# Loading the first MLP weight's 128 half rows as the kernel's very first transfer, into a tile of their own

## Chip, cores and metric

The kernel runs on one core of a Trainium2 chip. The metric is the device time of one execution in microseconds. The time before is 189.7 us, the median of 3 runs (189.7 to 190.16).

## What is computed

A decode step for 8 batch rows: attention over the last 1024 cached positions, and an MLP, mixed by a gate.

```python
# x: 8 x 1 x 448; k_cache, v_cache: 8 x 8 x 4096 x 256; wq: 448 x 4096; wo: 4096 x 448
q = (x @ wq).reshape(B, Sq, 16, 256).transpose(0, 2, 1, 3)
k = repeat(k_cache[:, :, Sk - W:, :], 2, axis=1)          # W = 1024
v = repeat(v_cache[:, :, Sk - W:, :], 2, axis=1)
p = softmax(einsum("bhqd,bhkd->bhqk", q, k) * 256 ** -0.5)
a = einsum("bhqk,bhkd->bhqd", p, v).transpose(0, 2, 1, 3).reshape(B, Sq, 4096) @ wo
h = gelu(layernorm(x) @ w1 + b1)                          # w1: 448 x 1792
b = h @ w2 + b2                                           # w2: 1792 x 448
out = sigmoid((x * gate_w).sum(-1)) * a + (1 - sigmoid(...)) * b
```

All tensors are bfloat16.

## The kernel before

**The work.** `query` (L384) multiplies x by wq. Then, per batch row b, `transpose_keys` (L352) turns that row's keys on TensorE (a part by DVE and POOL, `turn_blocks`, L337), `scores` (L430) multiplies them by the query, the steps `top`, `expo`, `turn`, `scale` and `bring` make the softmax, and `values` (L502) multiplies the weights by the values. At the end `mlp_hidden` (L551) computes the MLP's hidden layer, and a last run of matmuls (L661 to L686) multiplies it by w2, and the attention's output by wo, into one sum.

**The loads.** Nearly everything large goes through one ring of four slots (`RING`, L69) of 32 KB per partition. `plan` is the list of loads in order: wq, the keys of row 0, then keys and values of each row in turn, `w12` (w1, and later w2), the last values, and wo (L162 to L177). `pump` (L98) issues loads as long as a slot is free, and `done` (L104), called when a slot's last reader is in place, issues the next. All of these are issued by SP, in this order, each as a few DMAs: `rows_loader` (L137) copies pieces side by side, `half_loader` (L115) and `pair_loader` (L125) load keys and values. Only x and the gate's weights are issued by ACT (L182, L186), and SP issues the biases between loads (L190). The order of instructions is written by hand (`manual_schedule`, L80); the framework adds the semaphore waits. A DMA takes one of a few completion semaphores in turn ("lanes"), so that a load also waits for an older load of its lane.

**The 448 rows of a weight.** 384 of them are three rows per partition, which load as one block. The remaining 64 rows are cut into halves, so that 128 half rows fill 128 partitions: `wq_t` (4096 B per partition) and `w1_t` (1792 B, L150). The matmuls over half rows use a stationary operand of their own (`ends`, L327): L402 for the query, L568 for the MLP. In the kernel before, slot `w12` holds w1's block, then w1's half rows from element `OW1T`, then w2 from element `OW2` (L153, L154). w2 is loaded behind the last values (`last_values`, L158).

Of the kernel before, what the change touches and what calls it, by code (L numbers as in the profile page):

```python
# [11 lines left out]
BF16 = mybir.dt.bfloat16  # L12
# [5 lines left out]
def kernel(  # L18
# [15 lines left out]
    nc = tc.nc  # L34
    P = nc.NUM_PARTITIONS
# [18 lines left out]
    FQ = F // QD  # L54
    FB = FQ // BL
    HH = HD // 2
    FH = F // 2
# [23 lines left out]
    consts = ctx.enter_context(tc.tile_pool(name="consts", bufs=1))  # L81
# [16 lines left out]
    def pump():  # L98
        while len(slots) < min(len(plan), consumed[0] + RING):
            t = ring.tile([P, SLOT], BF16, tag="slot", name="slot")  # L100
            plan[len(slots)](t)
            slots.append(t)
# [5 lines left out]
    def add(key, loader):  # L108
        index[key] = len(plan)
        plan.append(loader)  # L110

    def slot(*key):
        return slots[index[key]]

    def half_loader(src, b):  # L115
        def load(t):
            for i in range(NG):
                v = src[b, i:Hkv:NG, kv_base:Sk, :].rearrange(
                    "a (s c) d -> s a (c d)", c=NCK
                )  # L120
                nc.sync.dma_start(t[:, i * HS : (i + 1) * HS], v)

        return load

    def pair_loader(src, b, cuts=1):  # L125
        def load(t):
            n = HS // cuts
            tv = t[:].rearrange("p (i n) -> p i n", i=NG)
            v = src[b, :, kv_base:Sk, :].rearrange("h (s c) d -> s h (c d)", c=NCK)
            for k in range(cuts):  # L130
                nc.sync.dma_start(
                    tv[:, :, k * n : (k + 1) * n], v[:, :, k * n : (k + 1) * n]
                )

        return load

    def rows_loader(pieces):  # L137
        def load(t):
            o = 0
            for ap in pieces:  # L140
                n = ap.shape[-1]
                nc.sync.dma_start(t[:, o : o + n], ap)
                o += n

        return load

    wq_m = A_wq[0:DM, :].rearrange("(p r) n -> p (r n)", r=NR)
    wq_t = A_wq[DM:D, :].rearrange("r (h n) -> (r h) n", h=2)
    w1_m = B_w1[0:DM, :].rearrange("(p r) f -> p (r f)", r=NR)
    w1_t = B_w1[DM:D, :].rearrange("r (h n) -> (r h) n", h=2)  # L150
    w2_v = B_w2.rearrange("(p c) n -> p (c n)", c=FB)
    wo_v = A_wo.rearrange("(q p j) n -> p q (j n)", p=P, j=J8)
    OW1T = NR * F  # L153
    OW2 = OW1T + FH  # L154
    wq_r = [wq_m[:, 0:HD], wq_m[:, HD : NR * HD]]
    OWQ = HD // 2

    def last_values(t):  # L158
        pair_loader(A_v_cache, NB - 1, 2)(t)
        nc.sync.dma_start(slot("w12")[:, OW2 : OW2 + FB * D], w2_v)  # L160

    add(("wq",), rows_loader([wq_t] + wq_r))  # L162
    add(("k", 0), half_loader(A_k_cache, 0))
    for b in range(1, NB):
        add(("k", b), (half_loader if b == NB - 1 else pair_loader)(A_k_cache, b))
        add(("v", b - 1), pair_loader(A_v_cache, b - 1))
    add(("w12",), rows_loader([w1_m, w1_t]))
    add(("v", NB - 1), last_values)
    cuts = [(q, 0, J8) for q in range(NQW - 2)] + [
        (NQW - 2, 0, 4),  # L170
# [7 lines left out]

    x_sb = consts.tile([NB, D], BF16)
    consts.tile([P, SHIFT], F32, name="shift")  # L180
    pump()
    nc.scalar.dma_start(x_sb[:], xf)  # L182
    g_b = consts.tile([NB, D], BF16)
# [139 lines left out]
    def stationary(a, r):  # L323
        o = (a * NX + r) * GAP + BL
        return flat[:, o : o + NB]

    def ends(a, x2):  # L327
        o = (a * NX + NR) * GAP
        m = GAP + NB + BL * x2
        o += 0 if x2 else BL  # L330
        return flat[:, o : o + m], m
# [219 lines left out]
    def mlp_hidden():  # L551
        nc.vector.memset(hp[:], 0.0)
        w = slot("w12")
        for r in range(NR):
            for t in range(QD):
                o = r * F + t * FQ
                nc.tensor.matmul(
                    hp[BL * t : BL * t + NB, :],
                    lhsT=stationary(1, r),
                    rhs=w[:, o : o + FQ],  # L560
                    start=(r == 0),
                    stop=False,
                    skip_group_check=True,
                )
        for x2 in range(2):
            lhsT, m = ends(1, x2)
            o = OW1T + x2 * FQ
            nc.tensor.matmul(  # L568
                hp[0:m, :],
                lhsT=lhsT,  # L570
                rhs=w[:, o : o + FQ],
                start=False,
                stop=(x2 == 1),
                skip_group_check=True,
            )
        z = work.tile([P, FQ], F32, tag="w0", name="z")
        nc.vector.tensor_tensor(z[:], hp[:], b1_b[:], op=ALU.add)
        za = work.tile([P, FQ], F32, tag="w1", name="za")
        nc.vector.tensor_tensor(za[:], z[:], z[:], op=ALU.mult)
        zb = work.tile([P, FQ], F32, tag="w2", name="zb")  # L580
        nc.vector.tensor_scalar(
            zb[:], za[:], 0.044715, 1.0, op0=ALU.mult, op1=ALU.add
        )
        nc.vector.tensor_tensor(za[:], zb[:], z[:], op=ALU.mult)  # L584
        nc.scalar.activation(zb[:], za[:], ACT.Tanh, scale=0.7978845608028654)  # L585
        nc.vector.tensor_scalar(za[:], zb[:], 1.0, 0.5, op0=ALU.add, op1=ALU.mult)
        nc.vector.tensor_tensor(zb[:], za[:], z[:], op=ALU.mult)
        zt = work.tile([P, FB, BL], F32, tag="w3", name="zt")
        nc.vector.transpose(zt[:], zb[:].rearrange("p (e c) -> p c e", c=FB))
        hs = consts.tile([P, FB, NB], BF16)  # L590
        nc.vector.tensor_tensor(
            hs[:],
            zt[:, :, 0:NB],
            oall[:].rearrange("p (o b) -> p o b", o=1).to_broadcast([P, FB, NB]),
            op=ALU.mult,
        )
        return hs
# [25 lines left out]
    for b in range(1, NB):  # L623
# [9 lines left out]
    spread(b - 1)  # L633
    bring(b)
    hs = mlp_hidden()
    values(b)
    finish(b)
# [5 lines left out]
    w = slot("wo")  # L643
    NCH = NQW * J8
    chunks = [
        (hs[:, c, :], w2[:, OW2 + c * D : OW2 + (c + 1) * D]) for c in range(FB)
    ] + [(oP[:, c % J8, c // J8, :], w[:, c * D : (c + 1) * D]) for c in range(NCH)]
# [13 lines left out]
    for i, (lhsT, rhs) in enumerate(wide):  # L661
# [4 lines left out]
            rhs=rhs,  # L666
# [9 lines left out]
    for i, (lhsT, rhs) in enumerate(narrow):  # L676
        k = part[i]
        for h in range(2):
# [4 lines left out]
                rhs=rhs[:, h * DO : (h + 1) * DO],  # L683
# [39 lines left out]
```

## Time and profile before

| | |
|---|---|
| median of 3 runs | 189.7 us (189.7 to 190.16) |
| profiled execution, its own time | 189.85 us |
| span in its profile | 188.1 us |
| PE busy | 119.9 us (64%) |
| DVE busy | 95.3 us (51%) |
| ACT busy | 90.8 us (48%) |
| POOL busy | 67.1 us (36%) |
| read from HBM | 77.69 MB, 413 GB/s over the span |
| w1's half rows | 1 DMA of 224 KB |

How to read the profile: all times are microseconds from the span's start, if they are not marked ns. The row of 40 digits gives an engine's busy share in 40 equal slices of the span, in tenths; 9 is 90% or more. The DMA row is the mean over the core's 16 DMA engines, and the row under it what they moved. Queue q1 is SP's, q10 ACT's, and q8 and q14 fetch instructions. A timeline line is: start, duration, engine, line, operation, output <- input, count, and in brackets how long the engine had been idle and what ended that. An "SPq" line is the issuing of a DMA, not the transfer. The chain that ended last is followed back from the last instruction, at each step to what released it. The trace also holds a record of each DMA packet: its start, duration, size and queue, though not its engine.

### The profile page before, as it was taken

Reading aid. Unit: us, or ns where it says so; the run is one execution under the profiler, and the core shown is the slowest. Engines: PE = TensorE matmul, PEld = TensorE weight load, DVE = VectorE, ACT = ScalarE, POOL = GpSimd, SP = SyncE. Lnnn points to the kernel's source line nnn. Section 1 sums busy time; section 2 is a strip of 40 time slices with the busy share of each in tenths; the row PEclk is TensorE's granted clock in tenths of the full one; section 3 lists DMA queues with packets and bytes.
Section 4 is the critical chain, followed back from the end, with each engine's and each line's share of the span. In section 5 each row is a group of like instructions: output and inputs, shape, how many; then the busy total and the mean of one; then the engine's idle time right before and its main releaser. Section 6 shows DMA issues by size and latency. Waiting matters only on the chain.

```text
span 188.1 us, 2798 instructions
## 1 busy us (share of the span) xinstructions
PE 119.9 (64%) x1103; PEld 78.7 (42%) x1104; DVE 95.3 (51%) x166; ACT 90.8 (48%) x115; POOL 67.1 (36%) x143
## 2 busy tenths in 40 slices
PE   0255078778778396890684959943968885353772
PEld 0013077476357135650663457614853662110221
DVE  7304543664287726840682228824763773762511
ACT  2003879489469426941295129820891994010000
POOL 8000075093069605800398029101991840000000
PEclk9999859969999759997599678996699999955899
DMA  6999999999999999999999999999999999999991
GB/s 219 446 422 435 432 432 425 435 428 428 432 434 425 427 428 428 439 425 428 428 439 422 439 425 432 428 435 425 432 428 435 428 428 419 417 427 441 413 396 42
DMA packets 6771, 77.85 MB, mean 414 GB/s; under 512 B 588, under 2 KB 1128, under 8 KB 1896
## 3 DMA queue, kind: packets, MB, share of 16 engines
q1 hardware_dynamic: 6712, 77.68, 97.1%
q8 instruction: 8, 0.13, 0.2%
q10 hardware_dynamic: 48, 0.02, 0.0%
q14 instruction: 3, 0.02, 0.0%
HBM read 77.69 MB, written 0.01 MB: 413 GB/s over the span
## 4 chain that ended last, share of the span: by engine, by line
DMA 77%; PE 10%; POOL 5%; DVE 3%; ACT 2%; issue 1%; SPq 0%; POOLq 0%; ACTq 0%; DVEq 0%
DMA slot<-in_A_k_cache_dram 51%; DMA slot<-in_A_v_cache_dram 12%; DMA slot<-in_A_wo_dram 9%; POOL kt L347 5%; DMA slot<-in_A_wq_dram 5%; PE ktp L371 5%; ACT kt L377 2%; DVE kt L379 1%; PE S_ps L436 1%; PE S_ps L390 1%; PE S_ps L402 1%; PE PO L507 1%; DVE EB L463 1%; DVE B L339 1%; PE S_ps L680 0%
## 5 line engine op out<-in xcount | busy, mean ns | idle before, releaser
L347 POOL COPY kt<-B 32x128 f32<-32x128 f32 (+1 forms) x128 | 62.8, 490 | 85.2 <-DVE B L339 72.0
L371 PE MATMUL ktp<-ident_f,slot 128*128 128x128 f32 x468 | 69.8, 306 | 32.5 <-DMA slot<-in_A_k_cache_dram 17.6
L377 ACT COPY kt<-ktp 128x1024 bf16<-128x1024 bf16 x77 | 72.6, 1031 | 25.3 <-PE ktp L371 25.1
L371 PEld LDWEIGHTS ktp<-ident_f,slot 128*128 128x128 f32 x468 | 59.3, 157 | 45.9 <-issue 17.9
L379 DVE COPY kt<-ktp 128x1024 bf16<-128x1024 bf16 x40 | 27.4, 685 | 17.7 <-PE ktp L371 17.5
L507 PE MATMUL PO<-slot,ET 128*16 128x512 bf16 x256 | 19.2, 447 | 7.3 <-DMA slot<-in_A_v_cache_dram 7.3
L436 PE MATMUL S_ps<-kt,qw 128*4 128x512 bf16 x256 | 18.4, 433 | 7.9 <-POOL kt L347 7.9
L454 ACT ACTIVATE E<-S_ps,nmx 128x1024 f32<-128x1024 f32 x8 | 8.9, 1115 | 24.8 <-DVE nmx L449 24.8
L449 DVE TENSOR_REDUCE nmx<-S_ps 128x1 f32<-128x1024 f32 x8 | 9.8, 1225 | 19.8 <-PE S_ps L436 19.8
L339 DVE STREAM_TRANSPOSE B<-slot 128x512 f32<-128x512 f32 (+1 forms) x8 | 7.3, 909 | 20.5 <-DMA slot<-in_A_k_cache_dram 20.5
L507 PEld LDWEIGHTS <-ET 128*16 128x16 bf16 x256 | 7.8, 101 | 17.9 <-issue 13.5
L436 PEld LDWEIGHTS <-qw 128*4 128x4 bf16 x256 | 6.2, 88 | 16.6 <-issue 11.5
L463 DVE STREAM_TRANSPOSE EB<-E 128x1056 f32<-128x1056 f32 x8 | 10.2, 1278 | 0.3
L390 PE MATMUL S_ps<-slot,xw 128*8 128x512 bf16 x24 | 2.9, 618 | 10.6 <-DMA slot<-in_A_wq_dram 10.6
L523 DVE STREAM_TRANSPOSE T<-PO 128x512 f32<-128x512 f32 x8 | 5.6, 704 | 3.7 <-PE PO L507 3.7
L490 DVE TENSOR_TENSOR ET<-sm,mask 128x512 bf16<-128x512 f32 x8 | 5.5, 692 | 3.4 <-PE sm L482 3.4
L415 DVE STREAM_TRANSPOSE qt<-qs 128x512 bf16<-128x512 bf16 x2 | 1.3, 690 | 9.9 <-ACT qs L412 9.9
L390 PEld LDWEIGHTS <-xw 128*8 128x8 bf16 x24 | 0.7, 100 | 11.9 <-issue 6.0
L412 ACT ACTIVATE qs<-S_ps 128x1024 bf16<-128x1024 f32 x1 | 1.0, 1024 | 8.5 <-PE S_ps L402 8.5
L585 ACT ACTIVATE zb<-za 128x448 f32<-128x448 f32 x1 | 0.6, 579 | 8.3 <-DVE za L584 8.3
L652 PE MATMUL warm<-slot,ident 128*128 128x512 bf16 (+1 forms) x11 | 4.0, 428 | 0.2 <-issue 0.2
L461 DVE RECIPROCAL E<-total 128x32 f32<-128x32 f32 x8 | 2.8, 344 | 1.4 <-ACT E L454 1.3
(81 smaller groups left out, 56.7 us busy)
## 6 DMA issues: line engine op xcount, KB each, us to landing
slot<-in_A_v_cache_dram SPq DMA_DIRECT2D x7, 4096.0 KB, 29.8
slot<-in_A_k_cache_dram SPq DMA_DIRECT2D x6, 4096.0 KB, 36.5
slot<-in_A_k_cache_dram SPq DMA_DIRECT2D x4, 2048.0 KB
slot<-in_A_v_cache_dram SPq DMA_DIRECT2D x2, 2048.0 KB
slot<-in_A_wq_dram SPq DMA_DIRECT2D x1, 2048.0 KB
slot<-in_A_wo_dram SPq DMA_DIRECT2D x2, 896.0 KB
slot<-in_B_w_dram SPq DMA_DIRECT2D x1, 1568.0 KB
slot<-in_B_w_dram SPq DMA_DIRECT2D x1, 1344.0 KB, 22.2
```

What stands on the lines that cost most here:

```text
L339: nc.vector.transpose(B[:].rearrange("p c w s a -> p (c w s a)"), kn[:, 0 : n * P],)
L347: nc.gpsimd.tensor_copy(words[BL * w : BL * (w + 1), :, 0:n, g * S8 : (g + 1) * S8, 0], B[BL * g : BL * (g + 1), :, w].rearrange("p c s a ...
L371: nc.tensor.transpose(words[:, c, :, 0], kn[:, o : o + P], ident_f[:])
L377: nc.scalar.copy(dst, src)
L379: nc.vector.tensor_copy(dst, src)
L436: nc.tensor.matmul(S_ps[BL * t : BL * t + UR, n * QN : (n + 1) * QN], lhsT=qw[:, j, b, t, rep * u : rep * u + UR], rhs=KT[u][:, t, n * CQ ...
L449: nc.vector.reduce_max(nmx[:], S_ps[:], axis=AXIS.X, negate=True)
L454: nc.scalar.activation(E[:, 0:W], S_ps[:], ACT.Exp, bias=soft.pop(b)[:], scale=1.0, accum_out=total[:],)
L463: nc.vector.transpose(EB[:].rearrange("p c r -> p (c r)"), E[:])
L490: nc.vector.tensor_tensor(ET[:].rearrange("p c u a r -> p (c u) a r"), sm[:] .rearrange("p k (o r) -> p k o r", o=1) .to_broadcast([P, NCK ...
L507: nc.tensor.matmul(PO[BL * t : BL * t + Hq], lhsT=ET[:, c].rearrange("p u a r -> p (u a r)"), rhs=vn[:, c], start=(c < QD), stop=(c >= NCK ...
L523: nc.vector.transpose(T[:, 0 : NG * n], PO[:].rearrange("p u (e j) -> p u j e", j=J8))
```

## The change

w1's half rows leave slot `w12`. They get a tile of their own, `w1_b` (128 partitions x 896 elements), and are loaded by the very first DMA that SP issues, ahead of wq's half rows and wq's two blocks. Slot `w12` then holds w1's block and, from where the half rows were, w2. The two matmuls at L568 read the new tile. Nothing else differs.

```diff
     OW1T = NR * F
-    OW2 = OW1T + FH
+    OW2 = OW1T
...
-    add(("wq",), rows_loader([wq_t] + wq_r))
+    def first(t):
+        nc.sync.dma_start(w1_b[:], w1_t)
+        rows_loader([wq_t] + wq_r)(t)
+
+    add(("wq",), first)
...
-    add(("w12",), rows_loader([w1_m, w1_t]))
+    add(("w12",), rows_loader([w1_m]))
...
     x_sb = consts.tile([NB, D], BF16)
     consts.tile([P, SHIFT], F32, name="shift")
+    w1_b = consts.tile([P, FH], BF16)
     pump()
...
             lhsT, m = ends(1, x2)
-            o = OW1T + x2 * FQ
             nc.tensor.matmul(
                 hp[0:m, :],
                 lhsT=lhsT,
-                rhs=w[:, o : o + FQ],
+                rhs=w1_b[:, x2 * FQ : (x2 + 1) * FQ],
```

## Prediction

> **What bounds the kernel now.** I read the page's slices first, then the DMA queues and the chain that ended last, then the SP timeline, the fine windows at both ends and the packet records. From the page, parts 2 and 3:
>
> ```profile
> PE   0255078778778396890684959943968885353772
> ...
> DMA  6999999999999999999999999999999999999991
> GB/s 219 446 422 435 432 432 425 435 428 428 432 434 425 427 428 428 439 425 428 428 439 422 439 425 432 428 435 425 432 428 435 428 428 419 417 427 441 413 396 42
> ...
> q1 hardware_dynamic: 6712, 77.68, 97.1%
> ```
>
> The DMA engines are full in 38 of 40 slices, only the first and last are not, and SP's queue alone fills 97.1% of them. No compute engine is so. The chain that ended last says the same (page, part 4):
>
> ```profile
> DMA 77%; PE 10%; POOL 5%; DVE 3%; ACT 2%; issue 1%; SPq 0%; POOLq 0%; ACTq 0%; DVEq 0%
> ```
>
> Its PE and POOL pieces need care: they explain when SP *issued* a transfer, and that did not matter, as the SP timeline shows (start, duration, instruction):
>
> ```profile
> 0.73 1.35 SPq L142 DMA_DIRECT2D slot<-in_A_wq_dram  x3
> 2.12 1.27 SPq L121 DMA_DIRECT2D slot<-in_A_k_cache_dram  x2
> ...
> 15.42 0.60 SPq L131 DMA_DIRECT2D slot<-in_A_k_cache_dram  x1
> ...
> 46.93 0.65 SPq L131 DMA_DIRECT2D slot<-in_A_k_cache_dram  x1
> ...
> 139.87 0.82 SPq L142 DMA_DIRECT2D slot<-in_B_w_dram  x2
> 145.65 1.29 SPq L131 DMA_DIRECT2D slot<-in_A_v_cache_dram  x2
> 146.99 0.59 SPq L160 DMA_DIRECT2D slot<-in_B_w_dram  x1
> 154.98 21.54 SPq L142 DMA_DIRECT2D slot<-in_A_wo_dram  x8
> ```
>
> I added up what had been issued before each line and took off what had moved (steady rate 429 GB/s, from 16,384-byte packets of 611 ns on 16 engines; the 3.38 MB moved by 10 us put the effective start at 2.14 us). The smallest backlog is at 46.93: 24.64 MB issued, 19.2 MB moved, 12.6 us of work waiting. At 139.87 it is 17 us, at 154.98 19 us. So the engines never wait for SP, and the kernel is *ramp, plus all bytes, plus a short tail*. In the packet records I chained the packets into 16 sequences: from 8 us on no sequence has a gap above 9 ns. The end, from the timeline:
>
> ```profile
> 184.38 0.87 PE L680 MATMUL S_ps<-slot,oP 128*8 128x224 bf16 x12 [0.52 <-DMA slot<-in_A_wo_dram]
> 185.29 0.38 DVE L690 TENSOR_TENSOR res<-S_ps,early 64x224 bf16<-64x224 f32 x1 [1.22 <-PE S_ps L680]
> 185.70 0.32 SPq L692 DMA_DIRECT2D out_dram<-res  x1
> ```
>
> The last piece of wo sets it. The span is 188.1 us, this execution took 189.85 (1.75 lie around the span), and the median of the runs is 189.7.
>
> **The change, part by part.**
>
> *Bytes.* The load of w1's 128 half rows (128 x 1792 B = 0.23 MB) is the same in both kernels, only its place differs. The packet records give 74 ns per 1792-byte packet, 8 per engine. Tail: -8 x 74 ns = -0.59 us ahead of the last values. Front: +0.59 us ahead of wq. For the last byte of wo the sum is 0.
>
> *What becomes late in between.* Everything from wq's half rows to w1's block lands 0.59 us later. The query starts with wq's first block (6.80 to 7.4) and ends with the blocks (15.40 to 16.0), so the next key load is issued at 16.0 in place of 15.42; the backlog there is 24.6 us, so nothing starves. In the middle every issue slides by at most 0.59 us against 12.6 us of backlog. If that cover were gone, each such slide would cost its 0.59 us once.
>
> *The tail.* The values of batch 6 become usable at 159.5 in place of 158.91, and the MLP's vector chain follows at most 0.59 us later: its last step (L591) ended at 170.41 + 0.28 = 170.69 and would end by 171.3. It is needed with w2's landing at 176.22, so 4.9 us of slack remain. The last values have as many bytes ahead of them as before, and keep 167.5 and 172.5. Gain there: none; loss: none.
>
> *SP's queue.* SP still issues the same number of loads; one issue of about 0.41 us (the first wq piece's, from the chain) moves ahead of wq, k0, k1 and v0, and leaves the place after 140 us. In front, v0's issue slides from 4.09 to some 4.6. Semaphore lanes move by one load, so v0's issue now also waits for w1's half rows: they start at 1.86 and need 0.59 us plus one first-packet latency (0.31 to 0.85 us in the records), so they are down by 3.3 to 3.9, ahead of 4.6. Behind v0 nothing is queued until 16 us. At the end wo's third piece no longer waits for a lane and the next two wait for older loads than before; the last three wait for the same ones. Since 19 us were queued at 154.98, that is worth 0. The two matmuls at L568 read the new tile and lose their wait: 0.57 us of PE work, off the path. ACT's and POOL's queues are not passed.
>
> *The ramp.* This is the one term that can be other than 0. In the first 5 us the packets took 0.37 us per engine beyond their usual durations, 0.27 us of it in wq's half rows (128 packets, mean 193 ns against a median of 159). Those first-packet latencies are now met by 1792-byte rows. No row shows that. Lower end: all of it goes, -0.37. Upper end: the latency is met twice, by w1's rows and again by wq's, +0.27. The nearest row is wq's own half rows: after one slow packet the next ones run at full pace, so the latency is paid once whatever the row length. I take 0.
>
> Does the small first load run dry before the second arrives? Issues are 0.47 us apart (0.73 and 1.20 in the chain); w1's packets last 0.59 us per engine even without latency. So no gap. The Trainium skill speaks against the change here: "DMA: Bandwidth & Descriptors", section "Anatomy of one DMA", fits each DMA with about 2.0 us fixed plus its bytes, for DMAs that GpSimd issues. By that estimate a lone 0.23 MB load would be mostly overhead and the sum would be +2.0 us; the trace, with gaps of at most 9 ns between packets of successive loads, shows no such cost between loads that are queued.
>
> *The new tile.* It takes 1792 B per partition and moves the addresses of what is allocated after it. No row shows what that does. Compute could slow by its slack before anyone sees it: PE waits 17.6 us for keys over six batches, 2.9 us per batch of 19.5 us, and the 12.6 us of backlog on top. I take 0.
>
> *Sum:* -0.59 + 0.59 + 0 = 0, with -0.37 to +0.27 for the ramp: 189.85 on the profiled execution's footing, 189.5 to 190.1. It stands 0.15 above the median of the runs; I forecast 189.8.
>
> **Rivals.**
>
> 1. *An instruction fetch falls on an engine that already has one (slower).* The records show eight 16 KB instruction fetches (at 36, 53, 70, 86, 108, 126, 148 and 163 us), 0.88 to 0.97 us each, and the packet behind each took about 1.1 us in place of 0.61: 1.4 us on one engine. Eight of the 16 sequences end at 184.3 to 184.6, eight at 182.8 to 183.6, as if each fetch had an engine of its own, and the late ones set the end. If the moved load put two on one engine, the end would be 1.4 us later: 191.2. It decides as soon as one engine gets a second fetch. Against it: PE has 1282 rows in both orders, and the fetches come with PE's progress.
>
> 2. *The start is exposed (slower).* If w1's rows were through before wq's packets come, the engines would wait again. The first SP packet comes at 1.86, 1.13 us after its issue at 0.73, so at most that is lost: 190.9. It needs w1's rows to last under 0.47 us. For it: the windows show only 39 GB/s in the second microsecond. Against it: 0.59 is over 0.47.
>
> 3. *The ramp shrinks (faster).* ACT's x load had its first packet 0.96 us after its issue, SP's first 1.13. If small rows started like x's (-0.17) and met no latency (-0.37), the time would be 189.3; beyond that I see nothing to gain, as the bytes remain.
>
> 4. *The wq delay counts (slower).* If the query's 0.59 us passed through to the end it would give 190.4. Against it: the backlog of 12.6 us and more.
>
> **How the numbers follow.** About 0.3% (0.57 us) is what a measurement of this kernel can tell from no change. My forecast, no change, holds 0.60 (189.5 to 190.1). Rival 1: 0.07; rival 2: 0.08; rival 4: 0.07, of which a part would fall within 0.3%; rival 3: 0.10; what I have not thought of, for which the address shift and the launch stand, 0.08. Beyond 0.3%: faster 0.16 (the larger part of rival 3 and half of the unnamed), slower 0.22, the same 0.62. The range, 189.1 to 190.9, takes in the ramp's bounds and rivals 2 to 4, and leaves out rival 1 and the far unnamed.
>
> **What would show it.** Right: the first packets are w1's, wq's first block is used near 7.4 us and its blocks near 12.2, the query ends near 16.0, DMA slices stay at 9, w2's matmuls still start near 176.2 and the last wo matmuls near 184.4. Rival 1: one engine's packets end 1.4 us after the next. Rival 2: a low GB/s in the window 2.3 to 3.5 us. Rival 3: wq's first block used ahead of 7.1. Rival 4: a DMA slice under 9 in the middle. Wrong altogether: a last wo landing that moves although the slices are full.

## The result, and the profile after

The changed kernel took 191.62 us (median of 7 runs, 190.23 to 191.84), the kernel before beside it 189.77 us (189.61 to 190.16). The ratio is 1.0082, with a 95% interval of 1.0063 to 1.0101: slower. The profiled execution took 191.62 us, with a span of 189.9 us, 1.8 us more than before. The forecast was no change, 189.8 us, with a range of 189.1 to 190.9: wrong.

From the page of the changed kernel, parts 2, 3 and 4, the same lines as before:

```profile
PE   0017339959987385993396729961996988363892
...
DMA  6999999999999999999999999999999999999980
GB/s 205 357 435 442 438 421 424 431 435 438 431 418 426 430 435 428 428 431 428 431 435 428 435 421 438 431 435 425 424 435 431 435 421 426 419 425 436 414 354 15
...
q1 hardware_dynamic: 6712, 77.68, 96.6%
...
DMA 76%; PE 11%; POOL 5%; DVE 5%; issue 1%; SPq 1%; POOLq 0%; DVEq 0%
```

The digits say "full" in every slice but the first and the last two. The row under them does not: the second slice moved 357 GB/s, in the kernel before 446. Busy engines that move less are engines whose packets take longer. From the third slice to the 37th the two rows are alike. So the loss is made in the first 9.5 us. The windows show where. The columns are: stretch and its length, busy time of each engine, granted clock, DMA share, GB/s. First the kernel before, then the changed one:

```profile
2.00:4.00 2.00, 0.00 (x0) 0.00 (x0) 1.83 (x5) 0.95 (x1) 2.00 (x5) 1.00 0.93 354
4.00:6.00 2.00, 0.00 (x0) 0.08 (x1) 1.79 (x8) 0.00 (x0) 0.97 (x3) 1.00 1.03 420
6.00:8.00 2.00, 1.03 (x8) 0.24 (x9) 0.62 (x2) 0.29 (x1) 0.00 (x0) 1.00 1.04 442
```

```profile
2.00:4.00 2.00, 0.00 (x0) 0.00 (x0) 1.82 (x5) 0.95 (x1) 2.00 (x5) 1.00 0.99 357
4.00:6.00 2.00, 0.00 (x0) 0.07 (x1) 1.79 (x8) 0.00 (x0) 0.97 (x3) 1.00 0.92 315
6.00:8.00 2.00, 0.00 (x0) 0.01 (x1) 0.63 (x2) 0.29 (x1) 0.00 (x0) 1.00 1.00 365
```

Up to 4 us the two are equal. From 4 to 8 us the changed kernel moves 315 and 365 GB/s where it was 420 and 442, at a DMA share of 0.92 to 1.00. The packet records show two things in this stretch. First, engines wait inside packets: 8192-byte packets of wq's first block took up to 1.22 us; the usual duration is 0.31, and the longest before was 0.61. Second, some engines stand without any packet. wq's half rows are through on every engine by 4.43 us, but three engines start on wq's first block only at 5.57, 5.82 and 5.88 us, and their first packets then take 1.18, 0.99 and 0.80 us. Engines with a packet in flight, of 16:

| at, us | 4.0 | 4.5 | 5.0 | 5.5 | 6.0 |
|---|---|---|---|---|---|
| before | 16 | 16 | 16 | 16 | 16 |
| after | 16 | 12 | 13 | 13 | 16 |

From 4 to 9 us an engine stands without a packet for 0.37 us in the mean, in the kernel before for 0.00. The DMA share shows this only dimly, as it counts the whole of a packet in the window in which the packet starts. The use of wq's blocks, timeline of PE, before and after:

```profile
6.80 1.03 PE L390 MATMUL S_ps<-slot,xw 128*8 128x512 bf16 x8 [6.80 <-DMA slot<-in_A_wq_dram]
11.65 1.88 PE L390 MATMUL S_ps<-slot,xw 128*8 128x512 bf16 x16 [3.83 <-DMA slot<-in_A_wq_dram]
```

```profile
9.29 1.02 PE L395 MATMUL S_ps<-slot,xw 128*8 128x512 bf16 x8 [9.29 <-DMA slot<-in_A_wq_dram]
14.19 1.88 PE L395 MATMUL S_ps<-slot,xw 128*8 128x512 bf16 x16 [3.88 <-DMA slot<-in_A_wq_dram]
```

The first block is used 2.49 us later, not the forecast 0.59. SP's timeline:

```profile
0.73 0.40 SPq L163 DMA_DIRECT2D w_b<-in_B_w_dram  x1
1.19 1.36 SPq L142 DMA_DIRECT2D slot<-in_A_wq_dram  x3
2.59 1.26 SPq L121 DMA_DIRECT2D slot<-in_A_k_cache_dram  x2
3.90 1.79 SPq L131 DMA_DIRECT2D slot<-in_A_k_cache_dram  x1
5.74 0.79 SPq L131 DMA_DIRECT2D slot<-in_A_v_cache_dram  x1
17.95 0.60 SPq L131 DMA_DIRECT2D slot<-in_A_k_cache_dram  x1
...
149.62 1.28 SPq L131 DMA_DIRECT2D slot<-in_A_v_cache_dram  x2
```

The issue of k1 takes 1.79 us in the slow stretch; elsewhere it takes 0.60 to 0.65. The last values are issued at 149.62 instead of 145.65, 4 us later, and that costs nothing, as the backlog covers it. The end:

```profile
186.25 0.84 PE L684 MATMUL S_ps<-slot,oP 128*8 128x224 bf16 x12 [0.56 <-DMA slot<-in_A_wo_dram]
187.13 0.38 DVE L694 TENSOR_TENSOR res<-S_ps,early 64x224 bf16<-64x224 f32 x1 [1.22 <-PE S_ps L684]
187.53 0.32 SPq L696 DMA_DIRECT2D out_dram<-res  x1
```

It is the same end as before, 1.87 us later, and again the last piece of wo releases it.

**How a loss at 8 us reaches 186 us.** Every engine has the same bytes to move, and from 9 to 180 us it stands without a packet for only 0.06 us in the mean (before: 0.05), so what an engine loses at the start it has no slack to win back. The completion records (one per engine and load) say who lost. The 16 engines finished wq's first block at 5.94 to 6.39 us before. After, thirteen finished at 6.60 to 7.89 and three at 8.82 to 8.94: the three that had started late. The three are still behind when k0 is through: its second half completes at 20.53 to 20.97 before, at 21.75 to 23.53 after. At the end the 16 chained sequences finish at 182.8 to 184.6 before (mean 183.8) and at 183.4 to 186.5 after (mean 184.8). The mean engine lost 0.94 us, the last one 1.88, and the last one counts. The mean is about what the start shows: 0.37 us without a packet, and 0.61 us more inside packets than before (1.01 against 0.40 us per engine beyond the usual durations, in the first 10 us). The last engine's end is what an engine gives that lost some 1.9 us at the start and also had one of the eight instruction fetches: 183.1 + 1.9 + 1.4 = 186.4. The completion records bear this out: one of the three late engines (8.89 us at wq's first block) keeps its place from load to load until a completion that was due at 91.51 us comes at 92.92, 1.41 us late, with a fetch at 88.5. The next sequence ends at 185.64, so by this trace the loss would be about 1.0 us if that fetch had fallen on an engine that was not late (an estimate). That may be a reason why single runs differ (190.23 to 191.84); no trace shows it.

### The profile page after: what moved, and what is told of

It is laid out like the page before. It is cut to its first block, busy times and chain, and to the rows that moved or that the text cites. A ratio compares the mean times of both kernels' runs of the same rounds, so it can differ in the third digit from the quotient of the medians.

```text
span 189.9 us, 2799 instructions
## 1 busy us (share of the span) xinstructions
PE 123.7 (65%) x1104; PEld 80.0 (42%) x1104; DVE 95.0 (50%) x166; ACT 91.6 (48%) x115; POOL 66.7 (35%) x143
## 4 chain that ended last, share of the span: by engine, by line
DMA 76%; PE 11%; POOL 5%; DVE 5%; issue 1%; SPq 1%; POOLq 0%; DVEq 0%
DMA slot<-in_A_k_cache_dram 50%; DMA slot<-in_A_v_cache_dram 10%; DMA slot<-in_A_wo_dram 9%; DMA slot<-in_A_wq_dram 6%; POOL kt L352 5%; PE ktp L376 5%; DVE kt L384 2%; PE S_ps L441 2%; DVE B L344 1%; PE PO L512 1%; PE S_ps L395 1%; PE S_ps L407 1%; DVE EB L468 1%; PE S_ps L684 0%; SPq L142 0%
## 5 line engine op out<-in xcount | busy, mean ns | idle before, releaser
L376 PE MATMUL ktp<-ident_f,slot 128*128 128x128 f32 x468 | 73.2, 312 | 32.6 <-DMA slot<-in_A_k_cache_dram 19.2
L382 ACT COPY kt<-ktp 128x1024 bf16<-128x1024 bf16 x77 | 73.4, 1030 | 26.6 <-PE ktp L376 25.9
L376 PEld LDWEIGHTS ktp<-ident_f,slot 128*128 128x128 f32 x468 | 60.8, 161 | 47.5 <-issue 20.8
L512 PE MATMUL PO<-slot,ET 128*16 128x512 bf16 x256 | 17.4, 413 | 3.4 <-DMA slot<-in_A_v_cache_dram 3.4
L441 PEld LDWEIGHTS <-qw 128*4 128x4 bf16 x256 | 6.2, 87 | 15.9 <-issue 10.5
L417 ACT ACTIVATE qs<-S_ps 128x1024 bf16<-128x1024 f32 x1 | 1.0, 1024 | 11.0 <-PE S_ps L407 11.0
L656 PE MATMUL warm<-slot,ident 128*128 128x512 bf16 (+1 forms) x12 | 5.1, 527 | 0.0
L487 PE MATMUL sm<-EZ,perm 128*128 128x128 bf16 x8 | 1.9, 241 | 3.7 <-DVE EZ L474 3.7
```

The costliest lines, as they stand in the source:

```text
L376: nc.tensor.transpose(words[:, c, :, 0], kn[:, o : o + P], ident_f[:])
L382: nc.scalar.copy(dst, src)
L441: nc.tensor.matmul(S_ps[BL * t : BL * t + UR, n * QN : (n + 1) * QN], lhsT=qw[:, j, b, t, rep * u : rep * u + UR], rhs=KT[u][:, t, n * CQ ...
L512: nc.tensor.matmul(PO[BL * t : BL * t + Hq], lhsT=ET[:, c].rearrange("p u a r -> p (u a r)"), rhs=vn[:, c], start=(c < QD), stop=(c >= NCK ...
```

## The experiments

Eighteen kernels. The diffs are against the changed kernel where nothing else is said. "First block" is the time at which PE first uses wq's first block in the profiled execution. Each time stands beside that of the kernel before on the same chip, which was 189.72 to 189.84 us throughout.

### Which part of the change costs

**The new tile alone.**

```diff
+    def late(t):
+        rows_loader([w1_m])(t)
+        nc.sync.dma_start(w1_b[:], w1_t)
...
-    add(("wq",), first)
+    add(("wq",), rows_loader([wq_t] + wq_r))
-    add(("w12",), rows_loader([w1_m]))
+    add(("w12",), late)
```

> w1's half rows have a tile of their own but are loaded at their old place, behind w1's block. Theory 1 (the order of the first loads puts wq's first block into a stretch of slow packets between 4 and 9 us): no change, 189.7 +- 0.4, and wq's first block is used near 6.8 us. Theory 2 (the new tile's addresses slow the start or the DMA writes): all of the loss, 191.3, with the first block used near 9.3 us.

189.76 us, ratio 1.0002 (0.9992 to 1.0011), first block 6.81. The tile and its addresses cost nothing; the order of the loads is the cause.

**w1's half rows second.**

```diff
-        nc.sync.dma_start(w1_b[:], w1_t)
-        rows_loader([wq_t] + wq_r)(t)
+        nc.sync.dma_start(t[:, 0:n], wq_t)
+        nc.sync.dma_start(w1_b[:], w1_t)
+        nc.sync.dma_start(t[:, n : n + HD], wq_r[0])
+        nc.sync.dma_start(t[:, n + HD : n + NR * HD], wq_r[1])
```

> w1's half rows are loaded second: wq's half rows, w1's half rows, wq's blocks. Theory 1 in the form that any extra 0.23 MB ahead of wq's blocks moves them into the slow stretch: as the changed kernel, 191 to 191.8, first block used near 9.3 us. Theory 3 (what costs is that the very first packets are small, so that the engines leave the ramp out of step): 189.8 +- 0.4, first block used near 7.4 us. Theory 2 (addresses): 191.3.

191.59 us, ratio 1.0094 (1.0079 to 1.0109), first block 9.35. The loss is all there though the very first packets are those of before. Theory 3 falls in this form.

**w1's half rows behind v0.**

```diff
     pump()
+    nc.sync.dma_start(w1_b[:], w1_t)
```

> w1's half rows are loaded early but behind everything of the first round of loads (wq, k0, k1, v0), so that nothing moves ahead of v0. Theories 1 and 3: 189.7 +- 0.4, first block used near 6.8 us. Theory 2: 191.3.

189.76 us, ratio 1.0004 (0.9994 to 1.0013), first block 6.77. An early load of these rows is free if it comes behind the first round.

**No byte moved, wq's half rows in two loads** (against the kernel before).

```diff
-    add(("wq",), rows_loader([wq_t] + wq_r))
+    add(("wq",), rows_loader([wq_t[:, 0 : HD // 4], wq_t[:, HD // 4 : HD // 2]] + wq_r))
```

> The kernel before, with wq's half rows loaded in two DMAs of 2048 bytes per partition, so that the first packets are small and one more DMA stands in front, while no byte is moved. Theory 3 (small first packets): a loss of 0.5 us or more, 190.3 to 191.5, with slow 8192-byte packets between 4 and 9 us. Theory 1 (0.23 MB more ahead of wq's blocks): no loss, 189.8 +- 0.4. An extra issue of 0.4 us on SP alone, which both kernels share, would show as a loss here too.

191.83 us, ratio 1.0116 (1.0097 to 1.0135), first block 8.30 in its profile. w1 has nothing to do with it: the kernel before, with its first 512 KB cut in two, loses as much. The 0.23 MB ahead of wq (theory 1) are not needed.

### Is it SP's issuing, an extra load, or short packets?

**k1 and v0 held back** by a fill on VectorE that their issue waits for.

```diff
+    first_round = [2]
...
-        while len(slots) < min(len(plan), consumed[0] + RING):
+        while len(slots) < min(len(plan), consumed[0] + first_round[0]):
...
+        def held(t):
+            nc.vector.memset(t[0:32, 0:32], 0.0)
+            pair_loader(A_k_cache, 1)(t)
...
     moments()
+    first_round[0] = RING
+    pump()
     query()
```

> The changed kernel, with the issue of k1 and v0 held back until VectorE has finished its moments (near 6.7 us), by a small fill of k1's slot that VectorE writes first. Theory A (SP's issuing, slid back by one issue, collides with the engines' reading of wq's first block: the issue stalls and the packets go slow): the collision is smaller, wq's first block is used at 7.4 to 8 us, time 189.8 to 190.3. Theory B (small loads in front put wq's block into a slow stretch, whatever SP issues meanwhile): as the changed kernel, 191.2 to 191.8, first block near 9.3 us.

192.22 us, ratio 1.0119 (1.0101 to 1.0137), first block 9.38. SP issued nothing from 3.9 to 6.7 us, and the packets of 4.1 to 7 us were slow all the same, up to 1.44 us. Theory A falls: the long issue of k1 goes with the slow stretch and does not make it.

**A first load of 2 KB** that nobody reads (against the kernel before).

```diff
+    tiny = consts.tile([16, 64], BF16)
...
+        nc.sync.dma_start(tiny[:], B_w1[0:16, 0:64])
```

> The kernel before, with a load of 2 KB that nobody reads as the first DMA: one more issue on SP, no bytes to speak of. Theory A: the loss is there, 190.8 to 191.8. Theory B: nothing but the slid issue, 189.8 to 190.2. A theory that each extra load in front costs its fixed 0.4 to 0.5 us: 190.2.

191.79 us, ratio 1.0105 (1.0089 to 1.0121), which looked like theory A's loss; but the first block was used at 7.34 and no engine fell behind (wq's first block complete at 6.43 to 6.94). The loss was elsewhere: 16 KB packets took 615.6 ns in the mean, in the kernel before 612.2, all through the span. The small tile had moved the addresses behind it by 128 bytes. It was tried again further down.

**wq's two blocks as one load.**

```diff
-    wq_r = [wq_m[:, 0:HD], wq_m[:, HD : NR * HD]]
+    wq_r = [wq_m]
```

> The changed kernel, with wq's two blocks loaded as one DMA of 24 KB rows, so that k0, k1 and v0 are issued at the times of the kernel before and the number of loads ahead of them is the same again. Theory A: 189.8 +- 0.4. Theory B: 190.8 to 191.8. A theory that the 8 KB rows at a pitch of 24 KB are what is slow after small loads: 189.8 too, so that this run tells B from the others and e5 tells the others apart.

191.74 us, ratio 1.0096 (1.0078 to 1.0114). Neither the number of loads ahead of k0 nor the 8 KB rows at a pitch of 24 KB matter: here the rows are 24 KB without a gap, and three of them took 2.0 to 2.2 us (usual: 0.9 to 1.0). Two sequences ended at 186.6 and 186.9, the others by 184.6.

**w1's half rows issued by ScalarE.**

```diff
+    nc.scalar.dma_start(w1_b[:], w1_t)
+
     def biases():
```

> w1's half rows loaded early into their own tile, but issued by ScalarE behind x and the gate's weights; SP issues what it issued before, one issue fewer. Theory A: 189.8 +- 0.4. Theory B (extra small packets ahead of or among wq's): 190.5 to 191.5.

189.87 us, ratio 1.0007 (0.9996 to 1.0017), first block 7.27. ScalarE issued the load at 1.66 us, but the packet records have its packets at 5.19 to 9.93 us, among those of wq's blocks and behind wq's half rows. So the same small packets among wq's blocks are free, and theory B falls in that form. It is no test of the same load moved ahead of wq from the other queue.

**The half rows of wq by halves of the partitions** (against the kernel before).

```diff
+        for p in (0, P // 2):
+            nc.sync.dma_start(t[p : p + P // 2, 0 : HD // 2], wq_t[p : p + P // 2, :])
```

> The kernel before, with wq's half rows loaded in two DMAs of 64 partitions each: the packets stay 4096 bytes and their number stays, only one more DMA (and one more completion per engine) stands ahead of wq's blocks. Theory D (one more DMA of some size ahead of wq's blocks is enough): 191 to 192, packets of wq's first block up to 1 us, as in the run with two column halves (191.83). Theory E (it takes more or smaller packets ahead of wq's blocks: 16 and 2 completions per engine there, 8 and 2 here): 189.7 +- 0.4.

191.75 us, ratio 1.0100 (1.0085 to 1.0115). It fits theory D and is outside theory E's range. The first of the two loads ran at the usual 159 ns per 4096-byte packet once each engine's first packet was down; the packets of the second, from 3.1 us on, took up to 315 ns, and those of wq's first block up to 0.80 us. So here the slow stretch begins in the second load already.

**The half rows of wq as 256 packets of 2048 bytes in one load** (against the kernel before; quarter rows, so that 64 rows of wq enter in another order).

```diff
+        nc.sync.dma_start(
+            t[:, 0:n].rearrange("p (g n) -> p g n", g=2),
+            A_wq[DM:D, :].rearrange("r (h n) -> (r h) n", h=4).rearrange(
+                "(g p) n -> p g n", g=2
+            ),
+        )
```

> The kernel before, with wq's half rows loaded by one DMA of 256 packets of 2048 bytes (quarter rows, so that the last 64 rows of wq enter the query in another order than the reference's). Theory D: one DMA as before, 189.7 +- 0.4. Theory E: 16 packets per engine ahead of wq's blocks, 191 to 192.

189.97 us, ratio 1.0007 (0.9997 to 1.0016), first block 7.02. Short packets don't do it; two loads do. Theory E falls.

**The 2 KB load again, into a tile of 1792 bytes** (against the kernel before).

```diff
+    tiny = consts.tile([P, FH], BF16)
...
+        nc.sync.dma_start(tiny[0:16, 0:64], B_w1[0:16, 0:64])
```

> The run with a first load of 2 KB that nobody reads, now into a tile of 1792 bytes per partition instead of 128. In the earlier run the 16 KB packets took 615 ns in place of 611 all through the span, which at 0.65% of 181 us is 1.2 us, and the rest of its loss, some 0.5 to 0.8 us, was the slid issue. With the larger tile the packets should be at 611 again: 190.2 +- 0.3. If the addresses had nothing to do with it: 191.8 again.

190.39 us, ratio 1.0031 (1.0019 to 1.0043), first block 7.30. The 16 KB packets are back at a median of 611 ns. What is left, 0.55 us, is the slid issue: the engines have done the 2 KB at 1.9 us and wait for wq's packets until 2.2. The addresses cost the other 1.4 us.

**A first load of 64 KB** (against the kernel before).

```diff
+        nc.sync.dma_start(tiny[0:128, 0:256], B_w1[0:128, 0:256])
```

> A first load of 128 rows of 512 bytes that nobody reads (64 KB) ahead of the kernel before's loads. It has as many packets, DMAs and issues ahead of wq's blocks as the changed kernel, at two sevenths of the bytes. Theories D and E: 191 to 192, slow packets in wq's first block. A theory that bytes, that is the time the engines spend ahead of wq's blocks, decide: 190.0 to 190.4.

190.50 us, ratio 1.0037 (1.0022 to 1.0051), first block 7.37. Hardly more than the 2 KB load. Two loads ahead of the block are not enough, then; theory D falls as it stood. The first must have some size.

### Where the pair must stand

**The gate's weights later.**

```diff
     moments()
+    nc.scalar.dma_start(
+        g_b[:], gate_w.rearrange("(o d) -> o d", o=1).to_broadcast([NB, D])
+    )
     query()
```

> The changed kernel, with ScalarE's load of the gate's weights issued only after its work on the moments (near 7 us), so that no packet of ScalarE's queue falls between 2 and 7 us. Theory Q (an engine that turns from SP's queue to ScalarE's and back loses its read-ahead, and with short loads in front this falls on wq's half rows and first block): 189.7 to 190.2, first block used near 7.4 us. Every other theory: 191.2 to 191.8, near 9.3 us.

191.61 us, ratio 1.0098 (1.0080 to 1.0116), first block 9.37. ScalarE's load of the gate's weights (its packets now at 10.5 to 11.3 us) is not the cause; its load of x, through by 1.9 us, was left. Two sequences ended at 186.2 and 186.6, the other fourteen by 184.7.

**k0 ahead of wq's blocks.**

```diff
+    def second(t):
+        half_loader(A_k_cache, 0)(t)
+        n = HD // 2
+        nc.sync.dma_start(slot("wq")[:, n : n + HD], wq_r[0])
+        nc.sync.dma_start(slot("wq")[:, n + HD : n + NR * HD], wq_r[1])
```

> The changed kernel, with k0's two loads between wq's half rows and wq's blocks: w1, wq's half rows, k0, wq's blocks. The query comes some 10 us later, within the backlog. Theory R (it is the reading of wq's blocks that is slow): slow packets follow wq's blocks to some 14 us, or are gone if by then the engines are out of step; k0's packets stay at 611 ns. Theory S (it is the third load of any kind, or the time from 4 to 8 us): k0's packets take up to 1.2 us between 4 and 8 us, 191 to 192.

192.13 us, ratio 1.0116 (1.0063 to 1.0170). Now k0's packets are slow, up to 1.66 us in place of 0.61. Its windows (same columns):

```profile
4.00:6.00 2.00, 0.00 (x0) 0.08 (x1) 1.79 (x8) 0.00 (x0) 0.96 (x3) 1.00 1.04 354
6.00:8.00 2.00, 0.00 (x0) 0.00 (x1) 0.62 (x2) 0.29 (x1) 0.00 (x0) 1.00 0.96 377
8.00:10.00 2.00, 0.00 (x0) 0.00 (x0) 0.00 (x0) 0.00 (x0) 0.00 (x0) 1.00 0.97 410
```

The same dip at the same time, with other data of another tensor, so it is not wq's blocks. Whether the third place counts or the time from 4 to 8 us, this run alone doesn't tell. In the run with wq's half rows in two loads the third load was slow from 3.4 us on (8192-byte packets up to 1.40 us), which speaks for the place.

**k0, k1 and v0 held back.**

```diff
+    first_round = [1]
...
-        while len(slots) < min(len(plan), consumed[0] + RING):
+        while len(slots) < min(len(plan), consumed[0] + first_round[0]):
...
+    def held0(t):
+        nc.vector.memset(t[0:32, 0:32], 0.0)
+        half_loader(A_k_cache, 0)(t)
...
-    add(("k", 0), half_loader(A_k_cache, 0))
+    add(("k", 0), held0)
...
     moments()
+    first_round[0] = RING
+    pump()
     query()
```

> The changed kernel, with the issue of k0, k1 and v0 held back to some 6.7 us, so that SP issues nothing while wq's half rows and the start of wq's first block are read. Theory T (SP's issue of k0 from 2.6 to 3.9 us is what collides): 189.8 to 190.3, first block near 7.4 us. Otherwise: as the run that held k1 and v0 alone, 191.8 to 192.7.

191.27 us, ratio 1.0082 (1.0053 to 1.0111), first block 9.61, single runs from 189.96 to 192.47. With SP silent from 2.6 to 6.7 us the slow stretch is still there in the profiled run, and by their times in eight of the ten runs. Theory T falls.

**w1's half rows third.**

```diff
+        nc.sync.dma_start(t[:, 0:n], wq_t)
+        nc.sync.dma_start(t[:, n : n + HD], wq_r[0])
+        nc.sync.dma_start(w1_b[:], w1_t)
+        nc.sync.dma_start(t[:, n + HD : n + NR * HD], wq_r[1])
```

> The order wq's half rows, wq's first block, w1's half rows, wq's second block: everything ahead of the first block is as in the kernel before. If the loss belongs to two short loads ahead of wq's first block: 189.8 +- 0.4, first block near 6.8 us. If it belongs to the number of loads ahead of k0: 191 to 192 with slow packets in the second block.

189.78 us, ratio 1.0004 (0.9995 to 1.0014), first block 6.73. No loss, with the same number of loads ahead of k0.

**w1's half rows very first, but wq's blocks directly behind.**

```diff
+        nc.sync.dma_start(w1_b[:], w1_t)
+        nc.sync.dma_start(t[:, n : n + HD], wq_r[0])
+        nc.sync.dma_start(t[:, n + HD : n + NR * HD], wq_r[1])
+        nc.sync.dma_start(t[:, 0:n], wq_t)
```

> w1's half rows are the very first load, as in the changed kernel, but wq's two blocks follow directly and wq's half rows come last of wq. Theory U (two short loads, 0.22 to 0.5 MB each, one behind the other at the start, make the load behind them slow; neither the first place nor the small packets do): 189.8 to 190.3, no packet of wq's blocks far over 0.6 us. Theory V (a short first load of more than some 0.1 MB is enough): 191 to 192.

189.89 us, ratio 1.0009 (1.0000 to 1.0019). Its SP and PE timelines:

```profile
0.73 0.40 SPq L164 DMA_DIRECT2D w_b<-in_B_w_dram  x1
1.20 0.41 SPq L165 DMA_DIRECT2D slot<-in_A_wq_dram  x1
...
3.94 0.62 SPq L131 DMA_DIRECT2D slot<-in_A_k_cache_dram  x1
4.60 0.63 SPq L131 DMA_DIRECT2D slot<-in_A_v_cache_dram  x1
```

```profile
6.11 1.03 PE L398 MATMUL S_ps<-slot,xw 128*8 128x512 bf16 x8 [6.11 <-DMA slot<-in_A_wq_dram]
```

The very first load is the changed kernel's, k1's issue is short again, and nothing is lost at the end. The 8 KB packets from 2.5 to 3.4 us were slow here as well (0.39 to 0.86 us), against the expectation; but no engine stood without a packet (0.00 us from 2.6 to 9 us), and no sequence ended after 184.62. A short first load of this size is harmless (the smaller ones above cost 0.55 and 0.66 us). Theory V falls.

**The same pair, behind a load of 1 MB.**

```diff
+        nc.sync.dma_start(t[:, n : n + HD], wq_r[0])
+        nc.sync.dma_start(t[:, 0:n], wq_t)
+        nc.sync.dma_start(w1_b[:], w1_t)
+        nc.sync.dma_start(t[:, n + HD : n + NR * HD], wq_r[1])
```

> The order wq's first block, wq's half rows, w1's half rows, wq's second block: the same pair of short loads, one behind the other, but behind a load of 1 MB. Theory U as it stands (the pair must stand at the start): 189.8 +- 0.4. A wider theory (two completions of 16 engines within 1.3 us slow the load behind them wherever they stand): 191 to 192, with slow packets in wq's second block.

189.98 us, ratio 1.0013 (1.0004 to 1.0022). The pair is harmless away from the start. Theory U stands. The starts side by side, by the loads on SP's queue in their order:

| first loads, KB | us |
|---|---|
| 512, 1024, 2048 (before) | 189.72 to 189.84 |
| 512, 1024, 224, 2048 | 189.78 |
| 224, 1024, 2048, 512 | 189.89 |
| 1024, 512, 224, 2048 | 189.98 |
| 2, 512, 1024, 2048 | 190.39 |
| 64, 512, 1024, 2048 | 190.50 |
| 512, 224, 1024, 2048 | 191.59 |
| 224, 512, 1024, 2048 (changed) | 191.62 |
| 224, 512, 3072 | 191.74 |
| 512 in packets of 2 KB, 1024, 2048 | 189.97 |
| 256, 256, 1024, 2048 (by columns; by partitions) | 191.83; 191.75 |
| 224, 512, 2048 of k0 | 192.13 |

What marks the kernels that lose 1.5 us or more by the order of their first loads is that engines stand without a packet. From 4 to 9 us this came to 0.10 to 0.78 us per engine in the profiles of all nine of them (the changed kernel and eight of the runs), and to at most 0.02 us in the other eleven profiles. Slow packets alone are no such mark: 8192-byte packets took up to 0.86 and 1.16 us in the last two runs, which lost 0.07 and 0.16 us.

No version beat the kernel before.

## Why the prediction was wrong, point by point

- **What bounds the kernel: right.** The DMA engines bound it, and a delay in the middle is free: the last values were issued 4 us later at no cost.
- **The bytes (-0.59 and +0.59): right in sum.** With the same rows third, or issued by ScalarE, the time is that of before.
- **The new tile at 0: right** (1.0002), by luck in the choice of its size, as the 128-byte tile showed.
- **"This is the one term that can be other than 0", the ramp, taken as 0 within -0.37 to +0.27: this step failed.** It was right that the ramp is the term, and wrong on its size and kind. Two pieces of the working failed. I concluded "So no gap" from the boundary between the first load and the second alone, and supported it with gaps "of at most 9 ns" that had been read from 8 us on, behind the ramp. And I reasoned "the latency is paid once whatever the row length" and bounded the term by a mean over 16 engines. Measured: there is no gap behind w1's rows (0.01 us per engine from 2.6 to 3.4 us), but one load later, behind wq's half rows, engines stood for 0.37 us in the mean and three of them for more than 1.1 us each; and packets went over their usual durations by 1.01 us per engine, in the kernel before by 0.40. The three engines lost some 2 us. The kernel ends with its slowest engine, not with the mean one, so 0.94 us in the mean became 1.88.
- **The +2.0 us for a fixed cost of a lone small load**, which the prediction set aside, is near the measured 1.85 us only by chance: with the same load first and wq's blocks directly behind it the time is 189.89.
- **SP's queue:** v0's issue was forecast at 4.6 and came at 5.74, since k1's issue took 1.79 us. No run shows that this did harm: with k1 and v0 held back to 6.7 us the loss is there all the same.
- **Rival 1** was not what happened: the last engine of the changed kernel had one fetch and a late start. (The other kernels that lost were not followed in this way.) But its picture, that one late engine sets the end, is how the loss was passed on. Its 1282 rows of PE are not to be found in the page, which counts 1103 matmuls and 1104 weight loads.
- **Rival 2** named the right place and kind, engines that wait again at the start, with a price of up to 190.9. Its condition was the wrong one: w1's rows did last long enough for the load behind them, and the engines ran dry one load later. What it describes itself comes with a shorter first load: 0.55 us with 2 KB.
- **Rival 3**, the ramp that shrinks, did not come: the first packet was earlier (1.75 in place of 1.86 us), but w1's rows met as much first latency as wq's had (0.28 against 0.27 us per engine).
- **Rival 4** is refuted by other runs: with w1's rows issued by ScalarE, wq's blocks were used at 7.27 and 12.50 (before: 6.80 and 11.65) and the next key load was issued at 16.26 in place of 15.42, at 189.87 us.
- **Among the signs** I had put "a low GB/s in the window 2.3 to 3.5 us" for rival 2; it came from 4 to 8 us, behind the second load. The sign for "wrong altogether", a later landing of wo while the slices are full, is what came.

**What stays open.** Shown is what it takes: two loads of 0.22 to 0.5 MB in a row at the start of SP's queue, and a longer load behind them. Some engines then stand without a packet, and packets take up to 1.7 us. Not shown is why; what the standing engines waited for is in no record. SP's issuing of k0, k1 and v0, ScalarE's load of the gate's weights, the tensor that is read, the row pitch and the packet size are excluded by the runs above. The memory's side, and the first use of a queue in an execution, were not tried. The loss varies from run to run (190.23 to 191.84 us in the changed kernel), and what makes it vary is not shown either.

## What to carry to other kernels

When DMA engines are busy from end to end, "the same bytes in another order" is free only if no engine falls behind: look at each engine's completions at the start, and at whether it has a packet in flight there, because the last engine sets the end. A gap measured in the steady state says nothing of the start. In this kernel the starts without a loss had one load of 224 or 512 KB at most ahead of the first of 1 MB; further small loads behind that one cost 0.2 us at most. And after adding a tile, look at the usual duration of the large packets: a shift of addresses by 128 bytes cost 1.4 us here.

## What the runs showed of the hardware

- **Unaligned tiles.** A tile of 128 bytes ahead of the others raised the median 16 KB packet from 611 to 615 ns; a tile of 1792 bytes did not. The Trainium skill, "DMA: Bandwidth & Descriptors", section "How a descriptor splits into AXI transactions", has an access split into pieces of 256 bytes that start at 256-byte boundaries; an estimate by it is 516 beats in place of 512 for 16 KB, or 0.8% more, and the trace agrees with 0.7%. The section speaks of reads; here it is the destination whose address moved.
- **Queued loads** followed one another without a fixed time between them from 8 us on (gaps of at most 9 ns in the kernel before). At the start they need not: three engines stood for more than 1.1 us between the second load and the third. The first packet came 1.13 us after SP began its first issue in the kernel before.
- **A DMA share of 1.00 at 365 GB/s.** The share counts an engine that waits inside a packet as busy; GB/s beside it tells the difference.
